# Second batch's convolutions split over ScalarE and POOL, weights' high parts on ScalarE, their stores on POOL's queue

## The chip, the cores and the metric

The kernel runs on one core of one Trainium2 chip. The metric is device microseconds of one execution. Engines are named as in the profile: PE (TensorE), DVE (VectorE), ACT (ScalarE), POOL (GpSimd), SP (SyncE, which only issues transfers here).

## The reference

Causal attention feeds a gated block, and that feeds a block with a trigonometric token mixer. Cut to what matters:

```python
# batch 4, 12 heads, 448 positions, head size 64; width 768
scores = q @ k.T / 8, causal mask; attn = softmax(scores); x = attn @ v
gate_pre[t] = sum_k conv_w[k] * x[t - 4 + k]         # 5 taps, per channel
h  = sigmoid(gate_pre) * (x @ w_val)
x2 = h @ w_out
theta = x2 @ w_theta
y  = w_tok_r @ (x2 * cos(theta)) + w_tok_i @ (x2 * sin(theta))
u  = x2 + y
out = u + max(u @ w_ch, 0)
```

The weights arrive as 64-bit floats. The kernel reads them as pairs of 32-bit words and makes 32-bit floats of them itself.

## The kernel before, in words

**Split precision.** A product of two matrices is made of three passes: each operand is written as a rounded high part and a low part (the rest), and high by high, high by low and low by high are added up in PSUM. So every activation and every weight needs a copy that rounds (`hi`) and a subtraction (`lo`).

**Stages.** The batches go through in turn. `attention()` is a generator of five steps per head; `dense(b)` is a generator over the four matrix products and the token mixer of batch b. The first batch's attention runs alone; then, while `dense(b)` advances, the loop at L705 also advances the attention of batch b+1 by a rate (`RATE`). So during `dense(0)` (from the first `hf` at 96.5 us to the next batch's first at 316.9 us) the second batch's attention runs, with its six pairs of heads g = 6 to 11, among them its convolutions. What the text calls order is settled when the program is built: a scheduler places each instruction on its engine's queue by its own estimate of times, and each engine then works strictly in that order, waiting where an input is not ready.

**Weights.** There are 24 weight strips (n = 0 to 23, six for each of four matrices), each in two halves g. While `dense(0)` runs, every strip is made once: `load_w` (SP, raw words), `stage_w` (three DVE passes at L153, L156 and L160 and one ACT pass at L159 turn 64-bit into 32-bit), `split_w` (`pool_hi` L104, then `pool_lo` L107 or, for the first half of `w_theta`, `dve_lo` L110), and then a store of high and low part to scratch memory (L227), from which the later batches fetch them (`fetch_w`, L234). `gemm` at L476 asks for the split of the next strip, the staging of the one after it and the load of a third, so a strip is loaded three products ahead. Raw words and split strips share one ring of eight buffers (tag `wb`): a buffer comes free when the product that reads it is done and its store has read it.

**Convolutions.** `attn_X1` (L419) normalises a pair's attention output into `xf`, and splits it; `attn_X2` (L434) makes the five-tap convolution, and a tanh follows at L454. `CONV_POOL[g]` says where it runs: on POOL as five multiplications and four additions, else on DVE as one multiplication (L449) and four multiply-adds (L451). Of the second batch's pairs, g = 9 and 10 are on POOL, and 6, 7, 8 and 11 on DVE.

**Copies of the transposed probabilities.** `attn_PT` (L335) copies four pieces of each head out of PSUM; piece 3 of batch b goes to DVE where `3 >= PT_DVE[b]`, else to ACT.

**Buffers that the change touches.** `tmp` is a tag with two buffers: the convolution's products `tp` use it, and so does `hf` (L525), the gated product of `dense`'s first stage.

Of the kernel before, what the change touches and what calls it, by code (L numbers as in the profile page):

```python
# [9 lines left out]
F32 = mybir.dt.float32  # L10
# [3 lines left out]
AF = mybir.ActivationFunctionType  # L14
ALU = mybir.AluOpType
# [7 lines left out]

X_SEG = 3
U_DVE = (0, 1, 1, 1)
PT_DVE = (2, 2, 0, 0)
K_DUP = (2, 2, 2, 2, 2, 2, 0, 0, 0, 0, 0, 0, 0, 0, 0, 1, 0, 1, 0, 0, 0, 0, 0, 0)
X_LO = (0, 0, 0, 0, 0, 0, 0, 0, 0, 0, 0, 0, 0, 0, 1, 0, 0, 0, 0, 0, 0, 0, 0, 0)
H_LO = (1, 0, 1, 0)
# [7 lines left out]
ABS_DVE = (1, 0, 0, 0)  # L37
PIN = 2
W_DVE = '0010'
A_TILES = (10, 14, 22, 28, 34, 40, 46, 52)  # L40
TOK_LOAD = (3, 5, 7, 9)
TOK_TURN = (12, 13, 14, 15, 16, 17, 18)
LAG = 3
RATE = ((1.027, 1.063, 1.027), (1.029, 1.029, 1.089), (1.03, 1.03, 1.01), (1.057, 0.994, 1.041))
CONV_POOL = (1, 1, 1, 1, 1, 1, 0, 0, 0, 1, 1, 0, 0, 0, 1, 1, 0, 0, 0, 0, 1, 0, 1, 0)


@with_exitstack
def kernel(
# [14 lines left out]
    nc = tc.nc  # L64
    B, H, S, D = q.shape
    DM = H * D
    P = 128
# [4 lines left out]
    KW = conv_w.shape[0]  # L72
# [7 lines left out]
    pool = ctx.enter_context(tc.tile_pool(name="pool", bufs=2))  # L80
# [8 lines left out]
    cw = cpool.tile([P, KW, KC], F32, name="cw")  # L89
# [6 lines left out]
    def f32(ap):  # L96
        return ap.bitcast(F32)
# [5 lines left out]
    def pool_hi(dst, src):  # L103
        nc.gpsimd.tensor_scalar(out=dst, in0=src, scalar1=1.0, scalar2=0.0, op0=ALU.mult, op1=ALU.add)  # L104
# [9 lines left out]
    def exp_set(*args, **kw):  # L114
        exps.append(nc.scalar.activation(*args, **kw))  # L115
# [60 lines left out]
    def tok_chunk(m):  # L176
        pt = psum("tr")
        for c in range(NC):
            t = tok_raw[c]
            src = t[:CP, m * P : (m + 1) * P]  # L180
            nc.tensor.transpose(pt[:, c * CP : (c + 1) * CP], src, ident[:CP, :CP])
        nc.scalar.copy(wtok_h[:, m, :], pt[:, :S])
        dve_lo(wtok_l[:, m, :], pt[:, :S], wtok_h[:, m, :])

    stages = [w_val, w_out, w_theta, w_ch]
    scratch = dram.tile([NW, 2, P, 2 * KH * P], F32, name="scratch")
# [20 lines left out]
    def split_w(n, g):  # L207
        if n >= NW:
            return
        t = bits.pop((n, g))[:, :, 0].bitcast(F32).rearrange("p (c n) -> p c n", n=P)  # L210
        if n < AHEAD:
            hi, lo = (
                pool.tile([P, S], F32R, tag=tag, name="w_ahead", bufs=12)[:, : KH * P].rearrange("p (c n) -> p c n", n=P)
                for tag in ("act_hi", "act_lo")
            )
        else:
            hl = pool.tile([P, 2, KH, P], F32R, tag="wb", name="w_hl", bufs=8)
            hi, lo = hl[:, 0], hl[:, 1]
        pool_hi(hi, t)
        (dve_lo if int(W_DVE[n // KC]) > g else pool_lo)(lo, t, hi)  # L220
        if B > 1 and n < AHEAD:
            for a, x in enumerate((hi, lo)):
                nc.sync.dma_start(
                    out=scratch[n, g][:, a * KH * P : (a + 1) * KH * P], in_=f32(x.rearrange("p c n -> p (c n)"))
                )
        elif B > 1:
            nc.sync.dma_start(out=scratch[n, g], in_=f32(hl.rearrange("p a c n -> p (a c n)")))  # L227
        splits[n, g] = (hi, lo)

    def fetch_w(n, g):  # L230
# [104 lines left out]
    def attn_PT(i, kcs):  # L335
# [11 lines left out]
        for kc in kcs:  # L347
# [3 lines left out]
            t = pool.tile([CP, n], F32, tag=f"pt{kc}", name="pt", bufs=2)  # L351
            if kc % 2 and kc >= PT_DVE[i // H]:
                nc.vector.tensor_copy(t, src)
# [16 lines left out]
    def attn_X(g):  # L370
        if not 0 <= g < B * NP:
            return
        attn_X1(g)
        attn_X2(g)
# [59 lines left out]
    def attn_X2(g):  # L434
        b, hp = divmod(g, NP)
        x = xf[g % 2]
        gt = pool.tile([P, S], F32, tag="gate", name="gate", bufs=6)
        if CONV_POOL[g]:
            tp = pool.tile([P, S], F32, tag="tmp", name="tp")
            nc.gpsimd.tensor_scalar(  # L440
                out=gt, in0=x[:, 0:S], scalar1=cw[:, 0, hp : hp + 1], scalar2=1.0, op0=ALU.mult, op1=ALU.mult
            )
            for t in range(1, KW):
                nc.gpsimd.tensor_scalar(
                    out=tp, in0=x[:, t : t + S], scalar1=cw[:, t, hp : hp + 1], scalar2=1.0, op0=ALU.mult, op1=ALU.mult
                )
                nc.gpsimd.tensor_tensor(out=gt, in0=gt, in1=tp, op=ALU.add)  # L447
        else:
            nc.vector.tensor_scalar(out=gt, in0=x[:, 0:S], scalar1=cw[:, 0, hp : hp + 1], scalar2=None, op0=ALU.mult)  # L449
            for t in range(1, KW):  # L450
                nc.vector.scalar_tensor_tensor(  # L451
                    out=gt, in0=x[:, t : t + S], scalar=cw[:, t, hp : hp + 1], in1=gt, op0=ALU.mult, op1=ALU.add
                )
        exp_set(gt, gt, AF.Tanh, scale=0.5)  # L454
        gates[b, hp] = gt
# [20 lines left out]
    def gemm(acts):  # L476
        n = wn[0]
        wn[0] += 1
        pt = psum("mm")
        for g in range(2):  # L480
            split_w(n + 1, g)
            stage_w(n + 2, g)
            load_w(n + 3, g)
            fetch_w(n + 3, g)
            whi, wlo = splits.pop((n, g))
            for kc in range(g * KH, (g + 1) * KH):
                xhi, xlo = acts[kc]
                for m, (a, x) in enumerate(((whi, xhi), (whi, xlo), (wlo, xhi))):
                    nc.tensor.matmul(  # L489
                        pt[:, :S], lhsT=a[:, kc % KH, :], rhs=x,  # L490
                        start=kc == 0 and m == 0, stop=kc == KC - 1 and m == 2,
                    )
            if g == 0:
                yield
        return pt
# [189 lines left out]
    for n in range(5 * (H + 1) + X_SEG + 1):  # L685
        next(at, None)
        if n == 5:
            setup_conv()
        if W_AT <= n < 5 * H:
            with tc.issue_after(ttr_ins[-1].ins):  # L690
                for at_n, (m, g) in zip(A_TILES, ((0, 0), (1, 0), (0, 1), (1, 1), (2, 0), (2, 1), (3, 0), (3, 1))):
                    if n == at_n - W_AT:
                        load_w(m, g)
                    if n == at_n:
                        stage_w(m, g)
                        if m < AHEAD + 1:
                            split_w(m, g)
        i, c = divmod(n, 5)
        if AHEAD and i >= 3 and i % 2 == 1 and c == A_SEG:
            gemm_ahead((i - 3) // 2)  # L700
        if n == 5 * H - 3:
            with tc.issue_after(ttr_ins[-1].ins):
                for g in range(2):
                    load_w(AHEAD + 2, g)
    for b in range(B):  # L705
        done = 0
        for y, _ in enumerate(dense(b)):
# [3 lines left out]
            if b == 0 and y in TOK_TURN:  # L711
                tok_chunk(TOK_TURN.index(y))
            r = RATE[b]
            y0 = max(0, y - LAG)
# [37 lines left out]
```

## Time and profile before

| what | us |
|---|---|
| median of three runs | 787.88 (785.45 to 790.54) |
| the profiled execution | 783.01 |
| its span in the trace | 781.2 |
| from the first `hf` of one batch to that of the next: batches 0, 1, 2 | 220.4, 176.8, 163.9 |
| the last batch, without attention beside it | 123.6 |

The profile's page gives each engine's busy time over the whole span, a digit for each fortieth of it, and the chain of work that ended last. Batch 0's dense part is the longest, and it is the one in which the changed work lies, so the views of the trace are taken there: busy time of each engine in stretches, groups of instructions with their mean duration, waits, and the chain in order of time. A wait says which engine stood idle, and what it was released by. The granted clock (PEclk) is a share of TensorE's full 2.4 GHz.

### The profile page before, as it was taken

How to read it: one execution, taken by the hardware profiler on the slowest of the kernel's cores; microseconds unless marked ns; L12 is line 12 of the kernel's file. 1: busy time of each engine (PE TensorE's matmuls, PEld its weight loads, DVE VectorE, ACT ScalarE, POOL GpSimd, SP SyncE). 2: the span in 40 equal slices, each digit the busy share in tenths (PEclk: the TensorE clock that was granted, in tenths of full speed). 3: DMA queues.
4: the chain of work that ended last, by engine and by line, in shares of the span. 5: the costliest groups of instructions: out<-in, count | busy, mean ns of one | idle time of the engine just before them, and what ended most of it. 6: DMA issues, size and time to landing. Idle time of an engine off the chain costs nothing.

```text
span 781.2 us, 12060 instructions
## 1 busy us (share of the span) xinstructions
PE 714.5 (91%) x3989; PEld 607.4 (78%) x3989; DVE 475.6 (61%) x1131; ACT 432.6 (55%) x1008; POOL 295.9 (38%) x327
## 2 busy tenths in 40 slices
PE   5888978796988998999899899999899999999997
PEld 4566666684777887898698798798798798898996
DVE  4888799979796672563666563753766633115531
ACT  5888855746877453455877533455797432225401
POOL 0678855664445672332154610122143241201100
PEclk9999989998898999899999999999999999999999
DMA  9437448989564599688634188678733178774222
GB/s 239 120 109 213 107 139 269 243 285 205 168 143 116 83 230 288 190 140 254 145 68 103 29 186 210 187 164 223 161 49 98 33 134 255 207 215 141 81 76 77
DMA packets 145420, 124.63 MB, mean 160 GB/s; under 512 B 87855, under 2 KB 120397, under 8 KB 145357
## 3 DMA queue, kind: packets, MB, share of 16 engines
q1 hardware_dynamic: 145357, 123.86, 62.5%
q8 instruction: 32, 0.52, 0.3%
q14 instruction: 31, 0.25, 0.1%
HBM read 99.38 MB, written 24.44 MB: 159 GB/s over the span
## 4 chain that ended last, share of the span: by engine, by line
PE 53%; DVE 10%; DMA 8%; ACT 7%; issue 2%; POOL 1%; SPq 0%; ACTq 0%; DVEq 0%; POOLq 0%
PE ps_mm L489 31%; PE ps_mm L584 11%; DMA out_dram<-o 5%; PE ps_av L365 3%; PE ps_tr L342 2%; DVE gate L451 2%; PE ps_s L321 2%; PE ps_s L322 2%; DMA scratch<-w_hl 2%; ACT L557 1%; PE ps_tr L570 1%; DVE qs L110 1%; ACT prob L115 1%; DMA rb<-rows 1%; ACT L115 1%
## 5 line engine op out<-in xcount | busy, mean ns | idle before, releaser
L489 PE MATMUL ps_mm<-act_hi,w_hl 128*128 128x448 f32 x864 | 268.8, 373 | 3.4 <-DVE w_hl L110 1.7
L489 PEld LDWEIGHTS ps_mm<-act_hi,w_hl 128*128 128x128 f32 x864 | 162.6, 190 | 18.2 <-DVE w_hl L110 2.0
L489 PE MATMUL ps_mm<-act_lo,w_hl 128*128 128x448 f32 x432 | 158.9, 369 | 0.0
L323 DVE CUSTOM_DVE_ANT_0 ps_s<-ps_s,mask 112x112 f32<-112x112 f32 x192 | 86.1, 454 | 67.7 <-PE ps_s L322 55.3
L115 ACT ACTIVATE prob<-ps_s,negm 112x112 f32<-112x112 f32 x192 | 95.3, 498 | 57.4 <-DVE negm L323 54.8
L342 PE MATMUL ps_tr<-ident,prob 112*112 112x112 f32 x480 | 79.4, 273 | 12.2 <-ACT prob L115 5.8
L107 POOL TENSOR_TENSOR act_lo<-x2f,act_hi 128x448 fp32r<-128x448 f32 x36 | 42.7, 1187 | 125.6 <-ACT act_hi L503 64.1
L489 PEld LDWEIGHTS ps_mm<-act_lo,w_hl 128*128 128x128 f32 x432 | 82.1, 191 | 5.1
L355 ACT COPY pt<-ps_tr 112x448 f32<-112x448 f32 (+2 forms) x120 | 51.9, 440 | 61.0 <-PE ps_tr L342 60.3
L489 PE MATMUL ps_mm<-x_hi,w_hl 128*128 128x448 f32 x264 | 81.5, 378 | 2.2 <-DVE hf L527 1.2
L321 PE MATMUL ps_s<-kk,qs 128*112 128x256 f32 x192 | 72.8, 383 | 11.0 <-ACT kk L308 2.9
L342 PEld LDWEIGHTS ps_tr<-ident,prob 112*112 112x112 f32 x480 | 57.5, 139 | 25.7 <-ACT prob L115 9.8
L584 PE MATMUL ps_mm<-wtok_h,zt_h 128*128 128x448 f32 x168 | 64.3, 383 | 2.8 <-ACT zt_h L575 2.6
L322 PE MATMUL ps_s<-klo,qs 128*112 128x256 f32 x192 | 62.8, 336 | 4.1 <-DVE klo L110 4.1
L584 PE MATMUL ps_mm<-wtok_h,zt_l 128*128 128x448 f32 x168 | 63.6, 379 | 0.1
L584 PE MATMUL ps_mm<-wtok_l,zt_h 128*128 128x448 f32 x168 | 62.4, 371 | 0.0
L365 PE MATMUL ps_av<-pt,v_raw 112*64 112x224 f32 (+3 forms) x384 | 58.9, 428 | 0.3 <-DVE klo L110 0.2
L447 POOL TENSOR_TENSOR gate<-gate,tp 128x448 f32<-128x448 f32 x48 | 56.5, 1177 | 2.7
L489 PEld LDWEIGHTS ps_mm<-x_hi,w_hl 128*128 128x128 f32 x264 | 50.7, 193 | 8.6 <-DVE hf L527 2.9
L107 POOL TENSOR_TENSOR x_lo<-xf,x_hi 128x448 fp32r<-128x448 f32 x23 | 28.2, 1224 | 67.0 <-ACT x_hi L430 66.5
L560 POOL TENSOR_TENSOR z<-z,x2f 128x448 f32<-128x448 f32 x18 | 20.6, 1145 | 86.3 <-ACT z L557 86.3
L365 PEld LDWEIGHTS ps_av<-pt,v_raw 112*64 112x64 f32 x384 | 28.2, 143 | 29.9 <-issue 17.4
(101 smaller groups left out, 1344.2 us busy)
## 6 DMA issues: line engine op xcount, KB each, us to landing
w_hl<-scratch SPq DMA_DIRECT2D x144, 384.0 KB, 3.9
scratch<-w_hl SPq DMA_DIRECT2D x44, 384.0 KB, 4.3
q_raw<-in_q_dram SPq DMA_DIRECT2D x48, 112.0 KB, 3.4
k_raw<-in_k_dram SPq DMA_DIRECT2D x48, 112.0 KB, 3.5
v_raw<-in_v_dram SPq DMA_DIRECT2D x24, 224.0 KB, 3.7
out_dram<-o SPq DMA_DIRECT2D x24, 224.0 KB, 3.3
cv_raw<-in_moe_w_val_dram SPq DMA_DIRECT2D x12, 384.0 KB, 4.6
cv_raw<-in_moe_w_out_dram SPq DMA_DIRECT2D x12, 384.0 KB, 5.2
```

What stands on the lines that cost most here:

```text
L107: nc.gpsimd.tensor_tensor(out=dst, in0=src, in1=f32(hi), op=ALU.subtract)
L115: exps.append(nc.scalar.activation(*args, **kw))
L321: nc.tensor.matmul(pt[:CP, :nn], lhsT=qs[:, cs], rhs=kk[:, :nn], start=True, stop=False)
L322: nc.tensor.matmul(pt[:CP, :nn], lhsT=qs[:, cs], rhs=klo[:, :nn], start=False, stop=True)
L323: ttr = nc.vector.tensor_tensor_reduce(out=pt[:CP, :n], in0=pt[:CP, :n], in1=mask[:, S - n : S], scale=-1.0 / math.sqrt(D), scalar=3.0e38, ...
L342: nc.tensor.transpose(pt[:CP, off : off + CP], prob[i, c][:, kc * CP : (kc + 1) * CP], ident[:CP, :CP])
L355: nc.scalar.copy(t, src)
L365: nc.tensor.matmul(av[g][j * D : (j + 1) * D, kc * CP : S], lhsT=tv[:, j, kc, :], rhs=pT.pop((2 * g + j, kc)), start=kc == 0, stop=kc == N ...
L447: nc.gpsimd.tensor_tensor(out=gt, in0=gt, in1=tp, op=ALU.add)
L489: nc.tensor.matmul(pt[:, :S], lhsT=a[:, kc % KH, :], rhs=x, start=kc == 0 and m == 0, stop=kc == KC - 1 and m == 2,)
L560: (nc.vector if Z_DVE[b] else nc.gpsimd).tensor_tensor(out=t, in0=t, in1=x2f[e], op=ALU.mult)
L584: nc.tensor.matmul(pt[:, :S], lhsT=a[:, m, :], rhs=w[:, m, :], start=m == 0 and n == 0, stop=m == NZ - 1 and n == 2,)
```

## The change

Four edits, all of which act in `dense(0)` and the second batch's attention beside it.

1. The convolutions of g = 6 to 11 (`CONV_ACT`): the five products by a tap's weight are made by ACT (a copy with a scale per partition), and the four additions by POOL. Each product after the first has its own `tp` buffer out of the two of `tmp`. Before, four of these six convolutions were on DVE and two on POOL.
2. The high parts of the strips n = 4 to 23 (40 halves) are made by `nc.scalar.copy` on ACT and not by POOL; n = 0 to 3 stay.
3. The stores of these 40 halves to scratch memory are issued from POOL's queue and not from SP's.
4. `PT_DVE[1]` goes from 2 to 4: piece 3 of the second batch's twelve heads is copied by ACT and not by DVE.

```diff
-PT_DVE = (2, 2, 0, 0)
+PT_DVE = (2, 4, 0, 0)
+W_HI = 4
+CONV_ACT = (0, 0, 0, 0, 0, 0, 1, 1, 1, 1, 1, 1, 0, 0, 0, 0, 0, 0, 0, 0, 0, 0, 0, 0)
 CONV_POOL = (1, 1, 1, 1, 1, 1, 0, 0, 0, 1, 1, 0, 0, 0, 1, 1, 0, 0, 0, 0, 1, 0, 1, 0)
...
-        pool_hi(hi, t)
+        if n < W_HI:
+            pool_hi(hi, t)
+        else:
+            nc.scalar.copy(hi, t)
...
-            nc.sync.dma_start(out=scratch[n, g], in_=f32(hl.rearrange("p a c n -> p (a c n)")))
+            (nc.sync if n < 4 else nc.gpsimd).dma_start(out=scratch[n, g], in_=f32(hl.rearrange("p a c n -> p (a c n)")))
...
-        if CONV_POOL[g]:
+        if CONV_ACT[g]:
+            nc.scalar.activation(gt, x[:, 0:S], AF.Copy, scale=cw[:, 0, hp : hp + 1])
+            for t in range(1, KW):
+                tp = pool.tile([P, S], F32, tag="tmp", name="tp")
+                nc.scalar.activation(tp, x[:, t : t + S], AF.Copy, scale=cw[:, t, hp : hp + 1])
+                nc.gpsimd.tensor_tensor(out=gt, in0=gt, in1=tp, op=ALU.add)
+        elif CONV_POOL[g]:
```

By count over the whole program: DVE loses 4 multiplications and 16 multiply-adds of 128x448 and 12 copies of 112x112. ACT gains 30 products of 128x448, 40 casts of 128x384 and 12 copies of 112x112, and its table loads in the program go from 38 to 36. POOL loses 10 multiplications and 40 casts, and gains 16 additions and 40 DMA issues. SP loses these 40 issues.

The order of the queues moves throughout `dense(0)`. In the changed file the same code has line numbers that are 2 to 11 higher. Three places matter to what follows.

ACT's queue in the first convolution of the second batch (g = 6, input `xf0`), before:

```order
L115 ACTIVATE prob_1780,sums_1344<-ps_s_1776,negm_1345 112x448
L300 CAST kk_1793<-ps_tr_1787 64x448
L430 CAST x_hi_1820<-xf0_72 128x448
L299 CAST qs_1799<-ps_tr_1782 64x448
L159 ACTIVATE cv_raw_1752<-cv_raw_1752 128x384
L536 ACTIVATE x2f_1965<-ps_mm_1905 128x448
```

and now:

```order
L117 ACTIVATE prob_1780,sums_1344<-ps_s_1776,negm_1345 112x448
L435 CAST x_hi_1820<-xf0_72 128x448
L444 ACTIVATE gate_1824<-xf0_72,cw_68 128x448
L447 ACTIVATE tp_1826<-xf0_72,cw_68 128x448
L447 ACTIVATE tp_1829<-xf0_72,cw_68 128x448
L224 CAST w_hl_1867<-cv_raw_1672 128x384
L547 ACTIVATE x2f_1887<-ps_mm_1839 128x448
L514 ACTIVATE act_hi_1889<-ps_mm_1839 128x448
L161 ACTIVATE cv_raw_1711<-cv_raw_1711 128x384
L305 CAST kk_1793<-ps_tr_1787 64x448
```

Three products and a weight's cast now stand between the softmax's last row block (`prob`) and the evacuation of the product (`x2f`, `act_hi`); the remaining two products come later, after POOL's first additions have freed their buffers.

POOL's queue at the same pair, before:

```order
L107 TENSOR_TENSOR act_lo_1882<-x2f_1879,act_hi_1881 128x448
L104 TENSOR_SCALAR w_hl_1906<-cv_raw_1711 128x384
L107 TENSOR_TENSOR w_hl_1906<-cv_raw_1711,w_hl_1906 128x384
L104 TENSOR_SCALAR kk_1793<-kk_1793 64x448
L107 TENSOR_TENSOR x_lo_1821<-xf0_72,x_hi_1820 128x448
```

and now:

```order
L109 TENSOR_TENSOR x_lo_1821<-xf0_72,x_hi_1820 128x448
L448 TENSOR_TENSOR gate_1824<-gate_1824,tp_1826 128x448
L109 TENSOR_TENSOR w_hl_1867<-cv_raw_1672,w_hl_1867 128x384
L109 TENSOR_TENSOR act_lo_1890<-x2f_1887,act_hi_1889 128x448
L448 TENSOR_TENSOR gate_1824<-gate_1824,tp_1829 128x448
L106 TENSOR_SCALAR kk_1793<-kk_1793 64x448
L232 DMA scratch_76<-w_hl_1867 128x768
L448 TENSOR_TENSOR gate_1824<-gate_1824,tp_1832 128x448
```

The casts of `w_hl` are gone, additions of the convolution stand between the low parts, and each weight's store (L232) has a place in POOL's queue, a few instructions behind its low part.

ACT's queue at the first two sine and cosine pairs of `dense(0)` (`z` is the angle's tile; a table load comes before the first sine after an exponential or tanh, and before the first of these after a sine), before:

```order
L115 ACTIVATE gate_2247<-gate_2247 128x448
L557 ACT_TABLE_LOAD
L557 ACTIVATE z_2295<-z_2295 128x448
L558 ACTIVATE z_2295<-z_2295,halfpi_69 128x448
L115 ACT_TABLE_LOAD
L115 ACTIVATE prob_2391,sums_2229<-ps_s_2387,negm_2230 112x336
L557 ACT_TABLE_LOAD
L557 ACTIVATE z_2370<-z_2370 128x448
L558 ACTIVATE z_2370<-z_2370,halfpi_69 128x448
L115 ACT_TABLE_LOAD
```

and now:

```order
L117 ACTIVATE prob_2407,sums_2237<-ps_s_2403,negm_2238 112x336
L117 ACTIVATE gate_2255<-gate_2255 128x448
L568 ACT_TABLE_LOAD
L568 ACTIVATE z_2311<-z_2311 128x448
L569 ACTIVATE z_2311<-z_2311,halfpi_69 128x448
L224 CAST w_hl_2410<-cv_raw_2280 128x384
L161 ACTIVATE cv_raw_2343<-cv_raw_2343 128x384
L568 ACTIVATE z_2386<-z_2386 128x448
L569 ACTIVATE z_2386<-z_2386,halfpi_69 128x448
L117 ACT_TABLE_LOAD
```

The row block `prob` of 336 columns now goes ahead of the first sine, so two pairs share one table load each way: two loads where there were four.

## Rows read from the trace of the kernel before

**Rows 1.** The page: the span, and each engine's busy us, share and instructions.

```profile
span 781.2 us, 12060 instructions
PE 714.5 (91%) x3989; PEld 607.4 (78%) x3989; DVE 475.6 (61%) x1131; ACT 432.6 (55%) x1008; POOL 295.9 (38%) x327
```

**Rows 2.** Stretch, length; busy PE, PEld, DVE, ACT, POOL; PEclk, DMA share, GB/s.

```profile
96.50:316.90 220.40, 192.74 (x1026) 158.87 (x1025) 174.31 (x392) 132.68 (x301) 117.72 (x136) 0.92 0.76 196
493.70:657.60 163.90, 158.01 (x913) 136.83 (x913) 90.56 (x223) 90.45 (x201) 44.31 (x45) 1.00 0.59 142
```

**Rows 3.** The same view inside batch 0's dense part.

```profile
96.50:140.00 43.50, 35.78 (x181) 28.94 (x180) 42.43 (x94) 24.81 (x59) 24.28 (x30) 0.92 0.72 216
140.00:250.00 110.00, 92.51 (x482) 75.02 (x481) 91.92 (x205) 76.40 (x164) 57.29 (x65) 0.89 0.73 189
...
190.00:200.00 10.00, 4.18 (x16) 2.22 (x16) 8.51 (x17) 9.89 (x15) 4.87 (x5) 0.74 0.49 172
```

**Rows 4.** L451 in four stretches (g = 6, 7, 8, 11): the last, the sum.

```profile
312.00:320.00 8.00, 4.12 (x4) 0.64 0.45 110
sum 48.00, DVE 13.98; mean DVE 3.50
```

**Rows 5.** L449 in the same four stretches.

```profile
312.00:320.00 8.00, 0.45 (x1) 0.64 0.45 110
sum 48.00, DVE 2.13; mean DVE 0.53
```

**Rows 6.** Groups by line, whole span: busy us, mean ns, idle before, releaser.

```profile
L353 DVE COPY pt<-ps_tr 112x112 f32<-112x112 f32 x48 | 12.9, 269 | 4.9 <-ACT pt L355 4.7
...
L159 ACT ACTIVATE cv_raw<-cv_raw 128x384 f32<-128x384 f32 x48 | 26.9, 563 | 14.9 <-DVE ps_cv L153 8.1 <-POOL gate L447 2.4 <-issue 2.3
...
L557 ACT ACT_TABLE_LOAD x19 | 24.4, 1283 | 0.3
...
L355 ACT COPY pt<-ps_tr 112x224 f32<-112x224 f32 x48 | 16.7, 349 | 18.1 <-PE ps_tr L342 17.9
...
L115 ACT ACTIVATE gate<-gate 128x448 f32<-128x448 f32 x24 | 13.8, 576 | 20.0 <-DVE gate L451 11.9 <-POOL gate L447 8.0
...
L447 POOL TENSOR_TENSOR gate<-gate,tp 128x448 f32<-128x448 f32 x48 | 56.5, 1177 | 2.7
...
L107 POOL TENSOR_TENSOR w_hl<-cv_raw,w_hl 128x384 fp32r<-128x384 f32 x38 | 40.5, 1066 | 2.3
L444 POOL TENSOR_SCALAR tp<-xf,cw 128x448 f32<-128x448 f32 x48 | 32.2, 670 | 2.7
...
L104 POOL TENSOR_SCALAR w_hl<-cv_raw 128x384 fp32r<-128x384 f32 x44 | 25.8, 587 | 57.4 <-DVE cv_raw L160 20.6 <-issue 10.1 <-ACT act_hi L505 5.4
```

**Rows 7.** The chain, 90 to 320 us: start, us, what.

```profile
190.24 0.54 ACT cv_raw L159
...
202.47 0.57 ACT z L558
...
206.95 2.60 DMA scratch<-w_hl
...
285.61 9.71 DMA scratch<-w_hl
```

**Rows 8.** Waits, 96.5 to 316.9 us: who waited for whom, us, times, longest.

```profile
POOL w_hl L104 <- DVE cv_raw L160: 18.1, 6, 7.0
...
POOL w_hl L104 <- DMA scratch<-w_hl: 5.2, 1, 5.2
...
DVE ps_cv L153 <- DMA cv_raw<-in_moe_w_theta_dram: 1.9, 2, 1.4
```

**Rows 9.** SP's queue: its waits, 96 to 316 us; then one store's issue.

```profile
SPq L227 <- POOL w_hl L107: 45.6, 20, 5.1
...
206.95 0.33 SPq L227 DMA_DIRECT2D scratch<-w_hl  x1
```

**Rows 10.** DMA issues, 96 to 316 us: count, KB each, us from issue to landing.

```profile
scratch<-w_hl SPq DMA_DIRECT2D x40, 384.0 KB, 4.4
```

## The prediction, made before the changed kernel had run

> **What bounds the kernel now.** I read the page first. PE is busy 91% of the span, no other engine over 61% [rows 1], so over the whole kernel PE bounds, and another engine counts only where it makes PE wait. Next the busy times by batch [rows 2]. Batch 0's dense part takes 220.4 us, with PE busy 192.7 us at a granted clock of 0.92, a mean of stretches at the full 2.4 GHz and at 1.2 GHz; batch 2's takes 163.9 us at 1.00, although two products more lie in it (batch 0's first two are made ahead). So some 50 us are lost in batch 0's part, and all four edits act there. DVE is busy 174.3 of its 220.4 us, more than ACT (132.7) and POOL (117.7). Third, the same view inside this part [rows 3]. From 96.5 to 140 us DVE is busy 42.4 of 43.5 us: full, with the weights' conversions. From 140 to 250 us DVE is busy 91.9 and ACT 76.4 of 110 us, and PE's clock is 0.89. In a piece of this (190 to 200 us) ACT is the full one, 9.9 of 10, and PE is busy 4.2. The reader is to see two engines that take turns as the bound, DVE first and ACT at the start of the theta products. After 250 us PE is nearly full.
>
> **The change part by part.** The sum is made against the profiled execution, 783.01 us (its span of 781.2 and 1.8 around it); the median of the runs is 787.88, a factor of 1.0062 more.
>
> *DVE's convolutions go.* The four together are busy 13.98 + 2.13 us [rows 4, 5]. The one for g = 11, at 312 us, is 4.12 + 0.45 and lies where DVE is not full, so it gives nothing. The three others lie between 141 and 226 us: 16.11 - 4.57 = 11.5 us off DVE. There DVE is the fullest engine, so I put them on the path: **-11.5** (ends: 0 if ACT's products take their place one for one, -16.1 with g = 11).
>
> *Piece 3's copies go.* 12 x 0.269 us [rows 6] = 3.2 us off DVE. The heads are spread evenly over the part, and half of it is the stretch from 140 to 250 us: **-1.6** (0 to -3.2).
>
> *Table loads.* The order shows two fewer at the first sines, where the chain runs through ACT without a break from 190.24 to 203.04 us [rows 7]. 2 x 1.283 us [rows 6] = **-2.6** (0 to -2.6; nothing else can turn up there that makes them longer).
>
> *SP's queue is freed.* SP stood 45.6 us waiting for POOL's low parts before it could issue a store, with loads queued behind [rows 9]. These loads run three products ahead, so they cover most of it; what was late shows as DVE waiting for a weight's words, 1.9 us [rows 8]: **-1.9** (0 to -1.9). Without this cover the whole wait would count.
>
> *ACT's new work.* 30 products at 0.576 us (the tanh of the same 128x448 tile is the nearest row) = 17.3; 40 casts at 0.563 us (the conversion's pass over the same 128x384 words) = 22.5; 12 copies at 0.349 us (the nearest, a piece of twice the columns) = 4.2 [rows 6]. That is 44.0 us in 220.4, or 0.20 us in each. Where ACT is the chain, 12.8 us, it costs 0.20 x 12.8 = **+2.6**. Ends: 0 if it all lies in ACT's waits, +22 if ACT becomes the bound from 140 to 250 us (half of 44). I take the row's share because ACT had 33.6 us free in that stretch [rows 3].
>
> *POOL.* It loses 40 casts (0.587), 10 multiplications (0.670), and gains 16 additions (1.177) [rows 6]: -23.5 - 6.7 + 18.8 = -11.4 us, to 106.3 of 220.4. The 40 issues come on top, and no row shows one from POOL. The nearest below is SP's issue of the same store, 0.33 us [rows 9]; above, 4.4 us, the time in which such a store is issued and landed [rows 10]. I take 1.07 us, POOL's own pass over the same strip's low part [rows 6], since POOL's instructions are the nearest thing that its queue runs: 43 us, so POOL stays at 149 of 220. On the chain a store stands twice, at 206.95 and at 285.61 us [rows 7]: 2 x 1.07 = **+2.1** (+0.7 to +8.8). Queued behind an issue on POOL are the next low part, and in the convolution the additions that free `tp`; who waits for these is the product two strips on and ACT's fourth and fifth tap.
>
> One rule of the Trainium skill speaks against this edit ("DMA: Bandwidth & Descriptors", section "SWDGE vs HWDGE vs iDMA"): descriptors of a DMA issued from GpSimd are computed in software and written to SBUF, and DVE locks GpSimd out of SBUF while it runs in its two-port mode. No run here shows it yet. If each of the two stores on the chain stood behind one such DVE pass, the sum would be higher by two passes of 0.45 us (a multiplication of one source) [rows 5], so under 1 us.
>
> *The buffers `tmp`.* The next batch's first `hf` now takes a buffer that POOL's additions for g = 11 must free. The product after it can run meanwhile in the second of the two accumulators, which covers it: 0. Without that cover it is four additions, 4.7 us [rows 6], once.
>
> The sum is -11.5 - 1.6 - 2.6 - 1.9 + 2.6 + 2.1 = -12.9 us. I do not take all of it. From 140 to 250 us ACT's 76.4 us would rise by half of the 44.0, less the 2.6 of tables: 95.8. At the fill that DVE reached in its fullest stretch, 42.43 / 43.5 = 0.975 [rows 3], this stretch can't get shorter than 98.3 us, so 11.7 is a ceiling there, and two engines that hand work to each other do not reach it. I take two thirds of the sum, **-8.6**: 774.4 us, which as a median is 774.4 x 1.0062 = **779 us**.
>
> **The rivals.**
>
> *ACT takes over as the bound (about no change).* DVE's stretch had 91.9 us of work in 110, a fill of 0.836. If ACT's 95.8 run at that same fill, the stretch takes 114.6 us: +4.6, 787.6, as a median 792.5. For it: the fullest engine is as full after as before. Against it: in the stretch DVE was full in pieces, with its passes back to back, and ACT's new passes can lie in ACT's waits.
>
> *The weight's cast blocks ACT (slower).* In this part POOL stood 18.1 us before its cast for DVE's last conversion pass, and 5.2 us for a store to free the buffer [rows 8]. The cast is now on ACT's queue, in strict order ahead of softmax pieces and evacuations (the first place of the order above), and so these waits would hold up the attention. The place is ACT's casts between 140 and 250 us; the price is 23.3 us less the 8.6 gained: +14.7, 797.7, as a median 803. It decides once the waits before these casts come to more than the gain, 8.6 us. Against it: the scheduler put the casts where it expects their input to be ready, and the waits stood on an engine that was idle in half the part.
>
> *POOL's issues are dear (slower).* With 106.3 us of work POOL fills the part once an issue costs more than (220.4 - 106.3) / 40 = 2.85 us. At 3.5 us POOL would need 246.3: +26, 809, as a median 814. The row that bounds it above, 4.4 us, counts the landing too, so I hold it unlikely.
>
> That the change does not do what it says is excluded by the order: the 40 issues, the casts and the products stand on the queues named.
>
> **How the numbers follow.** About 1%, or 7.9 us, is what a measurement of this kernel can tell from no change. The forecast has a chance of 0.53, ACT as the bound 0.27, the blocked casts 0.13, the dear issues 0.07. The forecast's case straddles the bound at 780.0: 0.41 of its 0.53 I count as faster by over 1%, as its ends (all of the sum; some of the lost clock given back) lie below, and 0.12 within. ACT as the bound: 0.04 faster, 0.18 within, 0.05 slower. The two others are slower, 0.20. Together: faster 0.45, within 1% 0.30, slower 0.25. Range: the lowest case is the full sum of -12.9 and half of the 17.6 us that the clock lost in this part (0.08 x 220.4) [rows 2], 761.3, as a median 766; the upper end, 801, takes in ACT as the bound and most of the blocked casts, and leaves out about 1 in 10 above. 766 to 801.
>
> **What would show it.** In the changed kernel's trace DVE from 140 to 250 us should fall by about 13 us, with no multiply-adds of the second batch's convolutions; ACT in batch 0's part should be near 174 us, and there should be two fewer table loads. The part itself should take about 212 us, the others as before. SP should hardly wait for POOL any more. I am wrong if ACT's casts show waits for DVE or for stores that come to over 9 us in all, if POOL shows long gaps at its issues with the low parts late and PE waiting for `w_hl`, or if the part is not shorter although DVE is freed: then ACT is the bound. A change in batches 1 to 3 would be none that I have priced.

## The result, and the profile after

The changed kernel takes 796.7 us (median of four, 793.5 to 798.8) against 788.9 for the kernel before in the same comparison: ratio 1.0119, interval 1.0078 to 1.016. It is slower; 779 us was forecast. The page of the changed kernel, span and busy times, against [rows 1]:

```profile
span 791.6 us, 12047 instructions
PE 716.5 (91%) x3989; PEld 608.8 (77%) x3989; DVE 463.1 (58%) x1099; ACT 464.7 (59%) x1088; POOL 305.6 (39%) x333
```

The span grew by 10.4 us. The stretches of the changed kernel, from the first `hf` of one batch to that of the next, and 140 to 250 us, with the columns of [rows 2]:

```profile
99.22:325.52 226.30, 191.09 (x1029) 160.17 (x1027) 164.07 (x369) 165.65 (x383) 126.96 (x143) 0.92 0.70 192
140.00:250.00 110.00, 91.77 (x496) 76.17 (x495) 82.20 (x183) 89.39 (x206) 68.72 (x77) 0.92 0.71 201
325.52:502.77 177.25, 170.25 (x988) 147.49 (x986) 98.14 (x236) 98.92 (x226) 58.29 (x55) 0.99 0.62 145
```

Batch 0's part went from 220.4 to 226.3 us, though DVE is busy 10.2 us less in it [rows 2]. PE is no busier and its clock is the same, 0.92: PE stands idle 35.2 us where it stood idle 27.7. The rest of the 10.4 us is 2.7 before the first `hf` (in the runs below that point lies anywhere from 95.9 to 101.3 us, so I read nothing into it) and under 2 in the later batches.

What the moved operations cost in the changed kernel, from the groups by line (busy us, mean ns, idle before and its releasers):

```profile
L109 POOL TENSOR_TENSOR w_hl<-cv_raw,w_hl 128x384 fp32r<-128x384 f32 x38 | 40.6, 1071 | 33.4 <-ACT w_hl L224 28.5 <-DVE x2f L633 2.0 <-PE ps_s L327 1.4
...
L448 POOL TENSOR_TENSOR gate<-gate,tp 128x448 f32<-128x448 f32 x24 | 28.2, 1176 | 2.1 <-ACT tp L447 1.4
...
L232 POOL DMA_DIRECT2D scratch<-w_hl x40 | 22.7, 568 | 14.4 <-DVE w_hl L112 7.1 <-POOL w_hl L109 3.9 <-ACT pt L360 2.5
...
L224 ACT CAST w_hl<-cv_raw 128x384 fp32r<-128x384 f32 x40 | 21.5, 544 | 7.1 <-PE ps_mm L500 4.3 <-DVE cv_raw L162 2.1 <-POOL w_hl L109 0.7
L447 ACT ACTIVATE tp<-xf,cw 128x448 f32<-128x448 f32 x24 | 15.5, 672 | 0.1
```

Each new operation costs about what was taken (the products 0.67 us where I took 0.58), a store's issue on POOL half of it (0.57 us). Behind the bars stand the waits: POOL's low parts wait 28.5 us for ACT's casts, and its stores 7.1 us for low parts that DVE makes. The first is in part an old wait in a new place: before, POOL stood 57.4 us at its own casts, 20.6 of it for DVE's last pass [rows 6]. POOL hardly waits for ACT's products (1.4 us). The waits from 99.2 to 327 us, for PE, DVE and SP's queue (who, for whom: us, times, longest):

```profile
PE ps_mm L500 <- DVE w_hl L112: 7.5, 2, 5.2
PE ps_mm L500 <- ACT w_hl L224: 6.2, 2, 5.4
...
DVE ps_cv L155 <- DMA cv_raw<-in_moe_w_theta_dram: 7.5, 5, 4.0
DVE ps_cv L155 <- DMA cv_raw<-in_moe_w_out_dram: 6.3, 3, 2.9
...
SPq L197 <- POOL w_hl L109: 40.5, 12, 6.9
SPq L197 <- DMA scratch<-w_hl: 19.2, 5, 10.4
...
SPq L197 <- DVE w_hl L112: 17.6, 4, 7.5
```

In the kernel before PE waited less for `w_hl`:

```profile
PE ps_mm L489 <- DVE w_hl L110: 1.7, 1, 1.7
...
PE ps_mm L489 <- POOL w_hl L107: 1.4, 2, 1.0
```

SP no longer stands at the stores (45.6 us [rows 9]), but now at the raw loads (L197), for buffers of the ring: the wait moved one instruction on. It is the same low part that ends it: the low part is the last pass that reads a strip's raw words, and so it frees the buffer into which a later load goes. (That a buffer waits for the product and the store holds for the split strips alone.) DVE's waits for raw words of `w_theta` went from 1.9 us [rows 8] to 7.5, and 6.3 for `w_out` came up. The place at which this reaches PE, in the changed kernel's timeline (start, us, engine, what; in brackets the idle time before it and its releaser):

```profile
185.59 18.44 SPq L197 DMA_DIRECT2D cv_raw<-in_moe_w_theta_dram  x5
...
191.48 1.16 POOL L448 TENSOR_TENSOR gate<-gate,tp 128x448 f32<-128x448 f32 x1
197.72 0.56 POOL L232 DMA_DIRECT2D scratch<-w_hl  x1 [5.09 <-DVE w_hl L112]
198.30 1.04 POOL L109 TENSOR_TENSOR w_hl<-cv_raw,w_hl 128x384 fp32r<-128x384 f32 x1
...
195.94 0.56 DVE L155 TENSOR_SCALAR ps_cv<-cv_raw 128x384 int32<-128x384 uint32 x1 [3.95 <-DMA cv_raw<-in_moe_w_theta_dram]
196.41 0.55 DVE L162 SCALAR_TENSOR_TENSOR cv_raw<-cv_raw,ps_cv 128x384 int32<-128x384 int32 x1
196.87 0.55 DVE L112 TENSOR_TENSOR w_hl<-cv_raw,w_hl 128x384 fp32r<-128x384 f32 x1
...
190.86 0.54 ACT L224 CAST w_hl<-cv_raw 128x384 fp32r<-128x384 f32 x1
...
196.54 0.56 ACT L161 ACTIVATE cv_raw<-cv_raw 128x384 f32<-128x384 f32 x1 [4.44 <-DVE ps_cv L155]
197.00 0.53 ACT L224 CAST w_hl<-cv_raw 128x384 fp32r<-128x384 f32 x1
...
197.48 1.11 PE L500 MATMUL ps_mm<-act_hi,w_hl 128*128 128x448 f32 x2 [5.18 <-DVE w_hl L112]
```

Read it from the bottom; which pass belongs to which strip follows from their order on each queue. PE stands 5.18 us for a low part that DVE makes at 196.87. It could have been made at 191.4, when ACT's cast for it (190.86) was done. But ahead of it in DVE's queue stands the first pass over a later strip, and that pass stands 3.95 us for its raw words, the load issued at 185.59. (The row's 18.44 us are the stretch over which SP issued five such loads, of which this is the first.) On ACT the cast of the next strip (197.00), whose words were ready at 189.1, stands behind ACT's pass over the same late strip (4.44 us). On POOL the store of the strip that PE waits for stands 5.09 us, and behind it is the low part of the next strip. One late load thus stops five queues, SP's with them, with ready work behind the waiting instruction on two of them, DVE and ACT. Before, the casts were on POOL, and the stores on SP.

The load itself was slow. The DMA issues from 184.4 to 191.4 us (count, KB each, median us to landing), and the DMA's share and GB/s in the middle of it (last two columns):

```profile
cv_raw<-in_moe_w_theta_dram SPq DMA_DIRECT2D x2, 384.0 KB, 10.3
...
rows<-rec SPq DMA_DIRECT2D x1, 3.5 KB, 8.5
```

```profile
186.00:190.00 4.00, 4.00 (x16) 3.50 (x15) 3.87 (x7) 1.44 (x5) 3.84 (x5) 0.57 0.35 34
```

The median over this part is 4.8 us for these loads. At 184.44 SP had issued `rows<-rec`, a pair's reciprocal sums on their way to memory, 3.5 KB, and it took 8.5 us. In the traces before, after and of the untied run with the stores from SP below, 39 weight transfers were issued in batch 0's part while such a transfer was under way, and all but one landed after it, with medians of 7.9 to 9.0 us against 4.4 to 4.9 for the others. Why is not shown. The kernel before has such slow loads too (one issued at 179.72 took 9.5 us), but there DVE did not wait for them.

### The profile page after: what moved, and what is told of

Its sections match the earlier page's. It is cut to its first block, busy times and chain, and to the rows that moved or that the text cites. A ratio compares the mean times of both kernels' runs of the same rounds, so it can differ in the third digit from the quotient of the medians.

```text
span 791.6 us, 12047 instructions
## 1 busy us (share of the span) xinstructions
PE 716.5 (91%) x3989; PEld 608.8 (77%) x3989; DVE 463.1 (58%) x1099; ACT 464.7 (59%) x1088; POOL 305.6 (39%) x333
## 4 chain that ended last, share of the span: by engine, by line
PE 57%; ACT 17%; DVE 11%; DMA 10%; issue 4%; POOL 2%; SPq 0%; DVEq 0%; ACTq 0%; POOLq 0%
PE ps_mm L500 29%; PE ps_mm L595 11%; PE ps_av L370 5%; DMA out_dram<-o 5%; PE ps_tr L347 3%; ACT prob L117 3%; PE ps_s L326 3%; PE ps_s L327 2%; DMA cv_raw<-in_moe_w_theta_dram 2%; DVE gate L462 1%; ACT pt L360 1%; DMA tok_bits<-in_moe_w_tok_i_dram 1%; DVE qs L112 1%; ACT L568 1%; DVE klo L112 1%
## 5 line engine op out<-in xcount | busy, mean ns | idle before, releaser
L500 PE MATMUL ps_mm<-act_hi,w_hl 128*128 128x448 f32 x864 | 271.6, 377 | 9.2 <-DVE w_hl L112 7.5
L500 PEld LDWEIGHTS ps_mm<-act_hi,w_hl 128*128 128x128 f32 x864 | 164.3, 193 | 23.2 <-DVE w_hl L112 8.3
L360 ACT COPY pt<-ps_tr 112x448 f32<-112x448 f32 (+3 forms) x132 | 53.6, 425 | 63.2 <-PE ps_tr L347 62.9
L370 PE MATMUL ps_av<-pt,v_raw 112*64 112x448 f32 (+3 forms) x384 | 59.6, 434 | 1.2 <-ACT prob L117 1.2
L571 POOL TENSOR_TENSOR z<-z,x2f 128x448 f32<-128x448 f32 x18 | 20.8, 1157 | 86.6 <-ACT z L568 86.5
L370 PEld LDWEIGHTS ps_av<-pt,v_raw 112*64 112x64 f32 x384 | 28.5, 145 | 32.7 <-issue 18.3
L109 POOL TENSOR_TENSOR w_hl<-cv_raw,w_hl 128x384 fp32r<-128x384 f32 x38 | 40.6, 1071 | 33.4 <-ACT w_hl L224 28.5
```

What stands on the lines that cost most here:

```text
L109: nc.gpsimd.tensor_tensor(out=dst, in0=src, in1=f32(hi), op=ALU.subtract)
L360: nc.scalar.copy(t, src)
L370: nc.tensor.matmul(av[g][j * D : (j + 1) * D, kc * CP : S], lhsT=tv[:, j, kc, :], rhs=pT.pop((2 * g + j, kc)), start=kc == 0, stop=kc == N ...
L500: nc.tensor.matmul(pt[:, :S], lhsT=a[:, kc % KH, :], rhs=x, start=kc == 0 and m == 0, stop=kc == KC - 1 and m == 2,)
L571: (nc.vector if Z_DVE[b] else nc.gpsimd).tensor_tensor(out=t, in0=t, in1=x2f[e], op=ALU.mult)
```

## The experiments

Each ratio is to the kernel before on the same chip, with its 95% interval. The scheduler orders the queues anew in every one of these kernels, so a difference of a few tenths of a per cent can be the order alone.

**DVE's relief by itself.** The kernel before, with g = 6, 7, 8, 11 left with the first tap only:

```diff
-            for t in range(1, KW):
+            for t in range(1, 1 if NP <= g < 2 * NP else KW):
```

> The kernel before, with the four multiply-adds of each DVE convolution of the second batch left out (g = 6, 7, 8, 11 keep the first tap only), so 16 DVE passes fewer and nothing in their place. My prediction's premise (DVE is the path from 140 to 250 us): 774 to 781 us. If DVE's convolutions are not on the path, or what is freed is taken back by the next wait: 784 to 791 us.

Measured 0.9854 [0.9779, 0.9928], 778.3 us; the part takes 210.3 us. So the relief is worth about 10 to 11 us when nothing takes its place (0.7 to 2.2% by the interval): the premise holds.

**ACT's work by itself.** The kernel before, with 30 products more:

```diff
+        if NP <= g < 2 * NP:
+            for t in range(KW):
+                nc.scalar.activation(dump, x[:, t : t + S], AF.Copy, scale=cw[:, t, hp : hp + 1])
```

> The kernel before with its convolutions as they were, and ACT making the 30 products besides, into a tile that nothing reads: 17 us of ACT work alone, with no wait on POOL. ACT theory (ACT's time itself is on the path): 794 to 802 us. Theory of the detour (not ACT's time but the new way by POOL's additions and the two buffers costs): no change, 786 to 792 us.

Measured 0.9964 [0.9936, 0.9992]. The products' time on ACT as such costs nothing.

**One edit at a time.** The stores alone (`nc.sync` to `nc.gpsimd` for n >= 4), the casts alone (`W_HI = 4`), the convolutions alone (`CONV_ACT`):

> The kernel before with one edit alone: the stores of strips 4 to 23 issued from POOL's queue. ACT theory (ACT's added work is the bound from 140 to 250 us): ACT's work is that of before, so no change, 786 to 792 us. Ring theory (a store issued from POOL goes out later, its buffer in the ring of eight comes free later, and SP's raw loads wait for it): most of the loss is here, 794 to 799 us, with SP's loads waiting for stores by 15 us or more.

> The kernel before with one edit alone: the high parts of strips 4 to 23 as casts on ACT. ACT theory: 22 us of the 44 us of new ACT work, half of the loss or more, 791 to 796 us. Theory of the late cast (the cast waits its turn in ACT's queue, so POOL's low part, the release of the raw buffer and the next raw load come later, however idle ACT is): the whole loss or more, 795 to 800 us, with POOL waiting for ACT's cast by 20 us or more. Ring theory: no change, 786 to 792 us.

> The kernel before with one edit alone: the second batch's convolutions as ACT products and POOL additions. My prediction's term: 11.5 us off DVE where it is full, so 777 to 785 us. ACT theory: DVE's gain and ACT's 17 us of products cancel, 786 to 792 us. Late cast and ring theory: DVE's gain shows, 777 to 786 us.

Measured 1.000 [0.9964, 1.0037], 1.0019 [0.9991, 1.0047], 1.0056 [1.0027, 1.0085]. Only the convolutions lose, and against the bare relief they lose 2%.

**One edit undone.** The change with the stores on SP, with the convolutions as before, and with the casts on POOL:

> The changed kernel with the stores put back on SP's queue, all else as changed. Ring theory: the loss goes, 785 to 790 us. ACT theory and the late cast: it stays, 794 to 800 us.

> The changed kernel with the second batch's convolutions put back as before (so ACT casts, stores from POOL and ACT's piece 3 stay). If the parts add up (convolutions alone +0.6%, casts alone +0.2%, stores alone 0): 790 to 794 us. If casts and products share one limit, ACT, so that the second costs more than it did alone: 787 to 791 us.

> The change with the casts back on POOL: split convolutions, stores on POOL's queue, copies on ACT. POOL then has the most work of all these kernels, and each low part follows its cast on one engine. If stores and additions on one queue are what costs, this is as slow as the change or slower: 1.010 to 1.022 (797 to 806 us). If the casts on ACT are what the convolution's loss is raised by, it falls back to the convolution alone: 1.002 to 1.008 (790 to 795 us).

Measured 1.010 [1.0042, 1.0158], 1.0004 [0.9977, 1.003], 1.0115 [1.0082, 1.0147]. With the convolutions as before nothing is lost; with them split, stores or casts raise the loss, and either is enough: with either one gone the loss stays near the whole (the interval of the first reaches down to that of the convolutions alone). The copies (`PT_DVE`) were not tried alone.

**The convolution's two halves, and the tie between them.** The convolutions alone, in three forms; the first:

```diff
-                tp = pool.tile([P, S], F32, tag="tmp", name="tp")
-                nc.scalar.activation(tp, x[:, t : t + S], AF.Copy, scale=cw[:, t, hp : hp + 1])
-                nc.gpsimd.tensor_tensor(out=gt, in0=gt, in1=tp, op=ALU.add)
+                nc.scalar.activation(dump, x[:, t : t + S], AF.Copy, scale=cw[:, t, hp : hp + 1])
+                nc.gpsimd.tensor_tensor(out=gt, in0=gt, in1=x[:, t : t + S], op=ALU.add)
```

The second keeps only the added `tensor_tensor` line, the third only the added `activation` line.

> The changed convolution alone (casts, stores and copies as before), with the tie between the two engines cut: ACT still makes the products after the first, but into a tile that nobody reads, and POOL adds the shifted input itself, so the taps' weights of four taps are left out. The work on ACT and on POOL, and DVE's relief, are those of the run with the changed convolution alone (1.0056 of before). If the tie is what costs (POOL waits for a product, ACT for a buffer of tmp), this run goes to what DVE's relief is worth with its cover: 0.985 to 0.993, some 777 to 783 us. If the work costs where it stands on the two queues, tie or not, it stays near 1.0056: 789 to 794 us.

> As the run before, without ACT's four later products: ACT makes the first product of each of the six convolutions, POOL adds the shifted input four times (four taps' weights left out). If POOL's additions, in strict order ahead of its low parts, are what takes DVE's relief back, this stays at 1.00 to 1.006 (788 to 793 us). If ACT's products are, it goes to 0.985 to 0.992 (777 to 782 us), as the run with DVE relieved and nothing in its place (0.985).

> The other half: ACT makes all five products of each of the six convolutions (four of them into a tile that nobody reads), and POOL adds nothing (four taps left out). If ACT's products, where the scheduler now puts them, take DVE's relief back, this stays at 1.00 to 1.006 (788 to 793 us). If they are free, as 30 such products were beside the convolutions of before (0.996), it goes to 0.98 to 0.99 (773 to 781 us), with POOL relieved of two convolutions as well.

Measured 0.9957 [0.9926, 0.9989], 0.9932 [0.9894, 0.9969], 0.9909 [0.9877, 0.9941]. Each half leaves about half of the relief's 1.5%, both without the tie leave 0.4%, and the tie turns that into a loss of 0.6%. The uncoupled run lies a little above the range that the tie's theory gave, and far below the other's. The wait itself is too short to be what costs: in the trace of the convolutions alone POOL and ACT hardly wait for each other:

```profile
L448 POOL TENSOR_TENSOR gate<-gate,tp 128x448 f32<-128x448 f32 x24 | 28.9, 1203 | 1.0 <-ACT tp L447 0.4
...
L447 ACT ACTIVATE tp<-xf,cw 128x448 f32<-128x448 f32 x24 | 15.5, 673 | 0.1
```

What is left is the order that the tie forces on the two queues, or the two buffers of `tmp`, which `hf` shares and which the uncoupled run leaves to it. The runs do not tell these apart.

**The convolutions wholly on POOL.** The kernel before with all four DVE convolutions on POOL, and with three of them:

```diff
-CONV_POOL = (1, 1, 1, 1, 1, 1, 0, 0, 0, 1, 1, 0, ...)
+CONV_POOL = (1, 1, 1, 1, 1, 1, 1, 1, 1, 1, 1, 1, ...)
```

> The kernel before with the second batch's four DVE convolutions on POOL, products and additions, and no new ACT work. ACT theory: DVE's gain shows, 777 to 785 us. Detour theory (POOL's additions stand ahead of its casts of the keys and of low parts): slower, 791 to 797 us. If DVE was not on the path and POOL is idle enough: 786 to 791 us.

> The kernel before with three more of the second batch's convolutions on POOL (g = 6, 7, 8), products and additions, and the last pair (g = 11) left on DVE, where DVE is not full. No tie between ACT and POOL, no new work on ACT. All four on POOL gave 0.996. If the last one, at the end of the part with the next batch's first product behind it, gives some of the gain back, this is 0.990 to 0.995 (781 to 785 us). If its place does not matter, 0.995 to 0.998 (785 to 787 us).

Measured 0.9956 [0.9927, 0.9985] and 0.9976 [0.995, 1.0002]; leaving the last pair on DVE does not help. The first is the fastest complete kernel of this study, by 0.4%, too little to call it a gain.

**The same convolutions on POOL inside the rest of the change**, with the stores on POOL's queue, and from SP:

> The change with the second batch's convolutions wholly on POOL (products and additions), and the rest of it kept: casts on ACT, stores on POOL's queue, copies. POOL is rid of 40 casts, and so has room for the four convolutions. If casts and products cost only because both stand on ACT, this gives what the convolutions on POOL gave alone or more: 0.990 to 0.996, 781 to 785 us. If a low part on POOL that waits for a cast on ACT is dear whatever else ACT does, it gives 1.00 or more, 788 us and above.

> The second batch's convolutions on POOL, casts on ACT, copies on ACT, but the stores issued from SP again. The same with the stores on POOL's queue was 1.019. If the stores are innocent (as 1.000 alone and 1.010 against 1.012 in the change say), this stays at 1.014 to 1.022 (799 to 806 us). If POOL's queue, standing at a store whose low part DVE makes (13.6 us in that run), is what costs there, it goes to 1.000 to 1.008 (788 to 795 us).

Measured 1.0194 [1.0159, 1.0229] and 0.996 [0.9929, 0.9991]. The second is below both cases of its expectation, and nearest the one in which POOL's queue is what costs: the place of the 40 stores is worth 2.3% here, and nothing alone. The first lies in its second case, but not for that case's reason, since the casts are on ACT in both. The first one's waits on POOL:

```profile
POOL w_hl L109 <- ACT w_hl L224: 41.6, 19, 6.3
POOL scratch L232 <- DVE w_hl L112: 13.6, 5, 7.3
```

In the second POOL waits even longer for the casts, 47.4 us, and it is fast. That points to the 13.6 us at the stores, which the second can't have; that it is these waits, and not the order that came with them, was not tried.

**The ties of the whole change cut.** First the cast's, then both, then both with the stores from SP:

```diff
-        (dve_lo if int(W_DVE[n // KC]) > g else pool_lo)(lo, t, hi)
+        (dve_lo if int(W_DVE[n // KC]) > g else pool_lo)(lo, t, hi if n < W_HI else t)
```

> The whole change, but the low part of the strips n = 4 to 23 is made from the 32-bit weight twice and not from the cast (it comes out as zero, so the low parts of these strips are left out): ACT makes the same casts, POOL the same subtractions, and POOL no longer waits for ACT there. If POOL's wait for ACT's casts (28.5 us in batch 0's part of the changed kernel) with all that stands queued behind it is what the casts cost, this goes from 1.012 to the run of the changed convolution alone, 1.003 to 1.007 (790 to 794 us), or below. If the casts cost by their own place on ACT, it stays at 1.010 to 1.014 (796 to 800 us).

> The whole change with both ties between ACT and POOL cut: low parts from the weight itself (zero), ACT's four later products into a tile that nobody reads, and POOL adding the shifted input (four taps' weights left out). The number of instructions on each engine is that of the change. If the two ties are the cause of the loss, this is at 0.988 to 0.998 (779 to 787 us), near the 0.996 of the untied convolution alone. If the sheer work on ACT and POOL is, it stays above 1.005 (792 us and more).

> The change with both ties cut (the same four taps' weights and low parts left out as there) and its stores issued from SP again. With them on POOL's queue it was 1.015. If the stores in POOL's queue, ahead of the low parts, hold the untied change up, this is at 0.992 to 1.001 (782 to 790 us), and a store's place on POOL costs wherever POOL is not slowed by something else. If the work put on ACT is what costs, ties and stores or not, it stays above 1.008 (795 us and more).

Measured 1.0073 [1.0047, 1.0099], 1.0148 [1.0114, 1.0183] and 0.9911 [0.988, 0.9942]. The first lies between its two cases. In its trace POOL stands no shorter at the low parts than in the change, now for DVE's last pass:

```profile
L109 POOL TENSOR_TENSOR w_hl<-cv_raw 128x384 fp32r<-128x384 f32 x34 | 29.1, 857 | 42.9 <-DVE cv_raw L162 28.8 <-DMA scratch<-w_hl 6.7 <-PE ps_mm L500 3.5
```

So the 28.5 us of waiting for casts are no price. (A subtraction of a tile from itself also takes POOL 0.86 us where it took 1.07, some 7 us in all: the runs with this tie cut have that much less work on POOL.) The second struck my theory that the ties alone are the cause: no tie, and no faster than the change. The third shows that the work as such is not: with the same instructions on ACT, DVE and PE and the same 40 stores, issued from SP, it is as fast as the forecast's case (780.4 us). Batch 0's part of the two (columns as above), first with the stores on POOL's queue, then from SP, each from its own trace:

```profile
97.70:327.44 229.74, 187.09 (x1017) 157.68 (x1016) 162.79 (x361) 163.43 (x377) 113.95 (x139) 0.90 0.71 188
```

```profile
99.70:309.04 209.34, 179.44 (x1018) 152.11 (x1016) 158.20 (x361) 162.25 (x376) 94.03 (x99) 0.95 0.76 206
```

ACT is as busy in the one as in the other, DVE 4.6 us less, POOL by the issues less, and 20.4 us lie between them: PE stands idle 12.8 us less in the second, and at a granted clock of 0.95 instead of 0.90 it is busy 7.7 us less. Where the idle time goes, in the timeline of the one with the stores on POOL's queue:

```profile
180.45 15.94 SPq L198 DMA_DIRECT2D cv_raw<-in_moe_w_theta_dram  x4
...
193.44 0.56 DVE L156 TENSOR_SCALAR ps_cv<-cv_raw 128x384 int32<-128x384 uint32 x1 [2.83 <-DMA cv_raw<-in_moe_w_theta_dram]
...
194.45 0.55 DVE L113 TENSOR_TENSOR w_hl<-cv_raw 128x384 fp32r<-128x384 f32 x1
...
185.81 1.14 POOL L448 TENSOR_TENSOR gate<-gate,xf 128x448 f32<-128x448 f32 x1
195.53 0.56 POOL L233 DMA_DIRECT2D scratch<-w_hl  x1 [8.59 <-DMA cv_raw<-in_moe_w_theta_dram]
196.11 0.84 POOL L110 TENSOR_TENSOR w_hl<-cv_raw 128x384 fp32r<-128x384 f32 x1
196.90 1.13 POOL L448 TENSOR_TENSOR gate<-gate,xf 128x448 f32<-128x448 f32 x1
197.99 1.13 POOL L571 TENSOR_TENSOR z<-z,x2f 128x448 f32<-128x448 f32 x1
...
208.35 1.76 PE L581 MATMUL ps_tr<-ident,z 128*128 128x128 f32 x7 [15.86 <-DVE z L570]
```

It is the place of the changed kernel's pile-up, the `w_theta` strips, of which DVE makes one low part in two. POOL stands 8.59 us at a store; the row names the load, and DVE's low part at 194.45, behind a pass that waits for words, comes last ahead of it. The next low part, the convolution's last addition and the token mixer's products (L571) are queued behind it; and PE stands 15.86 us at the transposes of `z`. The load that DVE waits for here was issued at 180.45, right behind a `rows<-rec` (180.04), and landed 12.9 us later.

The run with the stores from SP has slow loads at the same place (DMA issues from 184.4 to 191 us):

```profile
cv_raw<-in_moe_w_theta_dram SPq DMA_DIRECT2D x2, 384.0 KB, 11.9
```

But its loads run further ahead: these two are the tenth and eleventh of the twelve half strips of `w_theta`, where in the changed kernel they were the eighth and ninth, and DVE waits for neither. This fits a slow load that costs only where the loads have lost their lead.

The four cases of the whole change side by side:

| | stores from SP | stores from POOL's queue |
|---|---|---|
| ties between ACT and POOL | 1.0100 [1.0042, 1.0158] | 1.0119 [1.0078, 1.016] |
| both ties cut | 0.9911 [0.988, 0.9942] | 1.0148 [1.0114, 1.0183] |

Either is enough for the loss, and together they lose no more than one, which fits the pile-up above, where both hold up the same strips. In the case with ties and stores from SP POOL's wait for the casts is longer than in the change:

```profile
POOL w_hl L109 <- ACT w_hl L224: 47.3, 19, 8.3
```

Left open: how much of each step is the wait itself and how much the new order that the scheduler makes of it (no run moved one with the other held), and how much of the loss hangs on the slow loads (no run moved `rows<-rec`). That 47 us of this wait stand in a slow kernel and in a fast one (the convolutions on POOL, stores from SP) shows that it is not the sum of the wait that counts, but what is queued behind it; which of its 19 places is the dear one was not tried.

## Why the prediction was wrong

*DVE's convolutions, -11.5.* Right in size where nothing takes their place: the relief alone gave -1.5%, some 11 us. From 140 to 250 us DVE fell by 9.7 us (91.92 [rows 3] to 82.20), where about 13 were forecast.

*Copies and table loads, -1.6 and -2.6.* The table loads went as forecast: 36 in the program. Neither was tried alone, and neither shows in the time.

*SP freed, -1.9.* This is the step that failed on the side of the loads. "SP should hardly wait for POOL any more" was wrong: SP waited 40.5 us for POOL at the loads. I had looked at which instruction SP stood at, and not at what that instruction shares with the next: the load needs a raw buffer that the same low part sets free (40.5 us for POOL's, 17.6 for DVE's), or one that a store sets free when it lands (19.2 us).

*ACT, +2.6.* As time it is free (0.9964 for the products, 0.9911 for all of it without ties and with the stores from SP), and ACT did not become the bound: 165.7 us in the part (174 forecast), 89.4 of 110 in the stretch. The first rival falls.

*The casts block ACT.* They waited 7.1 us on ACT in all, under the 8.6 that I had set. The wait came on the other side of the hand-over: POOL's low parts stood 28.5 us for the casts. I priced what the cast waits for, not who waits for the cast. The length of that wait is no price either: 47 us of it stand in a fast kernel.

*The hand-overs.* **The step that failed.** The terms for ACT's work (+2.6) and POOL's issues (+2.1) charge each new instruction for the time that it takes where it is on the chain. What the instruction waits for in its queue, and the work that stands behind it there, is named without a price; the third of the sum that I left out, 4.3 us, is all that stands for it. The sizes were not at fault: an issue takes 0.57 us where I took 1.07, the rival by price (2.85 us and more) falls, and the work without the two ties and with the stores from SP (four taps' weights and the low parts left out) runs at 0.9911. The ties bring that to 1.0100, 1.9% or some 15 us; the stores' place on POOL's queue brings it to 1.0148, 2.4%; both together to 1.0119.

As for the stores alone: four pairs of runs differ in their place alone. In two of them it is worth 2.3 and 2.4%, in the changed kernel 0.2%, which is within the noise, and beside the kernel before nothing. So the issues on POOL's queue would have cost the gain, but taking them back does not save it. An issue that stands in order on POOL's queue waits for the strip it stores; for one half of each `w_theta` strip that part is finished on DVE. That wait was 7.1 us in the changed kernel and 13.6 in the run at 1.019. The prediction had named the sign, long gaps at POOL's issues with PE waiting for `w_hl`, and it came (5.09 and 5.18 us in the pile-up). The Trainium skill's advice to issue plain transfers from SP or ACT ("DMA: Bandwidth & Descriptors", section "SWDGE vs HWDGE vs iDMA") agrees with two of these pairs, and the two others show no difference. That section calls the setup without software the faster one; one issue did take less on SP, 0.33 us [rows 9] against 0.57, but that price shows in no time, since the stores alone gave 1.000.

*Two thirds of the sum, -8.6.* The case it describes exists: 780.4 us, with the ties cut and the stores from SP. That this is near 779 does not prove the sum, since DVE's relief by itself gives 778.3. The change as it is has both ties and the stores, and either gives it all back. The measured 796.7 us lies inside the range that I gave, 766 to 801, but its upper end was there for ACT as the bound and for casts that block ACT, and neither came.

## What to carry to other kernels

When work is split between two engines, ask for each queue that works in order: what does each new instruction wait for, and what stands behind it; a hand-over that costs 0.6 us of an engine's time can hold up everything after it. A transfer's issue belongs on the queue of an engine that has nothing to do behind it. And when a queue stands at one instruction for a buffer that others share, moving that instruction away can move the wait to the next one that needs the buffer. In these traces loads that ran well ahead hid a slow one; what ate their lead made it show.

## What the runs showed of the hardware

A store issued from POOL's queue takes POOL 0.568 us (mean of 40) against SP's 0.33 (one issue [rows 9]), and landed 5.0 us after its issue against 4.4 [rows 10]. While a `rows<-rec` of 3.5 KB was under way, for 8.5 us, the DMA engines moved 34 GB/s from 186 to 190 us, against 192 in the part's mean, and loads of 384 KB took 10.3 us. Thirty unread ACT products cost nothing and came out 0.4% faster, which is also one measure of what a new order of the queues alone can do here. Back to back, ACT's passes overlap: in the changed kernel a pass of 0.54 us began at 184.00 and the next one at 184.44, so busy time comes out below the sum of the durations.
